# Router rows turned by DMA transposes, and sums of squares added on TensorE, in a fused attention and two-layer mixture kernel

## The chip, the cores and the metric

The kernel runs on one core of a Trainium2 chip. The metric is the device time of the whole program in microseconds (us), lower is better. TensorE multiplies matrices and transposes through PSUM; VectorE, ScalarE and GpSimd work on SBUF (GpSimd does not touch PSUM); SyncE (SP) issues most of the transfers. Each engine works through its own queue in order and waits on semaphores of the others.

## What is computed

```python
a = softmax(scale * x @ state.T);  xread = a @ state        # 8 batches, 8 heads, 512 tokens, 32 states, 64 wide
a2 = softmax(scale * state @ x.T); sread = a2 @ x
t = concat(xread, sread)            # -> 4352 tokens x 512
h = t @ w_in;  y = leaky_relu(h, 0.01) @ w_out               # 512 -> 2048 -> 512
logits = y @ w_gate; e = argmax(logits); p = softmax(logits)[e]
g = sigmoid(y @ w_output_gate)[e]
out = p * g * (relu(y @ w1[e]) @ w2[e])                      # 8 experts, 512 -> 1024 -> 512
```

Inputs and output are float32. The kernel splits values in two parts (fp32r pairs in the first layer, fp16 pairs in the router and the experts) and multiplies high by high, high by low and low by high.

## The kernel before

The first layer runs in nine chunks: eight x chunks (c = 0 to 7), one batch of 512 tokens each, and one chunk of the 256 state tokens (c = 8). Each has 16 steps (f = 0 to 15), one for each 128 hidden features, numbered n = 0 to 143 over all chunks. The order of the work is written out by hand in one loop over n. In a step come, in this order: `mm1(n)` (hidden features, with ScalarE's scaled copy, VectorE's max, and a split into `gh` and `gl`), in chunk 0 a piece of the conversion of the weights from 64-bit form (`convert`), a piece of the next batch's attention (`attend`), one advance of the expert weights' split (`advance(pre)`), `mm2(n - 2)` (three matmuls for each of four token tiles, accumulated over the chunk in PSUM), and `pump()`, one advance of the router of the chunk before.

The split of the expert weights (`presplit`) goes over 32 jobs of two tiles each and has four stages a job. The first squares tile 0 on ScalarE (`squares`, line 93, with a sum for each partition); the second squares tile 1, and GpSimd adds the two sums into a bf16 column (`suw`, line 643); the third sums over the partitions by a matmul with ones on TensorE (`over_partitions`, line 138), from which VectorE makes a power of two (`norm_scale`), and splits tile 0 (`halve`: VectorE lines 625 and 626, GpSimd line 627); the fourth stores tile 0 and splits tile 1, which the next job's first stage stores. It begins at n = 14 with one stage a step; in the last x chunk, from f = 2 on, two stages are advanced in one step, both ahead of `mm2`.

The gates' weights are loaded at n = 2; `gate_weights` squares, sums and splits them at n = 14 (lines 141 to 149).

The router of a chunk begins when `mm2` of f = 15 has been issued, in step f = 1 of the next chunk. Copies and squares of y (`evacuate`) come first. Then, at one `pump` each: `halves` of tile 0, of tile 1; then, for each of the four tiles, the logits of the tile before, `turn` of the tile (8 transposes on TensorE into PSUM, one copy on ScalarE into `yT`), and `halves` two tiles ahead; then softmax, choice and a scatter of the rows into the sorted table in DRAM. `pump` comes once a step, twice in the state chunk from f = 3 on, and twice in each expert slot (37 slots of 128 rows follow the first layer). The router of c = 7 runs in the state chunk; that of the state tokens (two tiles) runs in the first slots.

The pool of tag "y" (`r_p`, two buffers) holds y of two token tiles at a time, and early on the raw pieces of w_in.

Of the kernel before, what the change touches and what calls it, by code (L numbers as in the profile page):

```python
# [9 lines left out]
FP32 = mybir.dt.float32  # L10
FP32R = mybir.dt.float32r
FP16 = mybir.dt.float16
BF16 = mybir.dt.bfloat16
I32 = mybir.dt.int32
ACTF = mybir.ActivationFunctionType
ALU = mybir.AluOpType
# [7 lines left out]
def tile_attention_moe_moe2(ctx, tc, x, state, w_in, w_out, w_gate, w_ogate, w1, w2, out):  # L24
    nc = tc.nc
    B, H, S, D = x.shape
    NS = state.shape[2]
    DM, FF = w_in.shape
# [64 lines left out]
    def squares(o, t):  # L93

        k, n = t.shape[1:]
        nc.scalar.activation(out=junk[:, 0:k * n].rearrange("p (k n) -> p k n", n=n), in_=t, func=ACTF.Square,
                             scale=2.0 ** 0.5, accum_out=o)

    def norm_scale(pool, ss, s, inv):

# [21 lines left out]
    gwl = const.tile([128, KD, 2 * E], FP16, name="gwl")  # L122
    ginv = const.tile([128, 2], FP32, name="ginv")
    gsc = const.tile([128, 2], FP32, name="gsc")
    gss = const.tile([128, 2], FP32, name="gss")
    gsa = const.tile([128, 2], FP32, name="gsa")
    gsb = const.tile([128, 2], BF16, name="gsb")
    einv = const.tile([128, 2, 2, E], FP32, name="einv")
    esc = const.tile([128, 2, 2, E], FP32, name="esc")

# [1 line left out]
        for i, w in enumerate((w_gate, w_ogate)):  # L132
            nc.sync.dma_start(gw32[:, i], w.rearrange("(k p) e -> p k e", p=128))

    def over_partitions(t):

        ps = psa.tile([128, t.shape[1]], FP32, tag="a", name="tot")
        nc.tensor.matmul(ps, ones16.bitcast(BF16), t, start=True, stop=True)
        return ps

    def gate_weights():
        for i in range(2):
            squares(gss[:, i:i + 1], gw32[:, i])
        nc.vector.tensor_copy(gsb, gss)
        nc.vector.tensor_single_scalar(out=gsa, in_=over_partitions(gsb), scalar=128.0, op=ALU.mult)
        norm_scale(const, gsa, gsc, ginv)
        for i in range(2):
            sl = slice(i * E, (i + 1) * E)
            parts16(gwh[:, :, sl], gwl[:, :, sl], gw32[:, i], gsc[:, i:i + 1])
# [224 lines left out]
    def advance(g):  # L374
        try:
            next(g)
            return True
        except StopIteration:
            return False
# [115 lines left out]
    def router(ys2, ss, rows, tok_cols):  # L495
# [10 lines left out]
            nc.gpsimd.tensor_copy(row[:, 2 * DM + 2:2 * DM + 4].bitcast(I32), tok_cols[t])  # L506

        def turn(t):
            pt = psa.tile([128, 2 * KD, 128], FP16, tag="a", name="pt16")
            for k in range(2 * KD):  # L510
                nc.tensor.transpose(pt[:, k, :], rows[t][:, k * 128:(k + 1) * 128], id16)
            yTs[t] = r_p.tile([128, 2 * KD, 128], FP16, tag="yT", name="yT", bufs=1)
            nc.scalar.copy(out=yTs[t], in_=pt)

        def logits(t):
            yT = yTs.pop(t)
            pl = psa.tile([128, 2 * E], FP32, tag="a", name="pl")
            n = 0
            for a, w in ((0, gwh), (0, gwl), (KD, gwh)):
                for k in range(KD):  # L520
                    nc.tensor.matmul(pl, yT[:, a + k, :], w[:, k, :], start=(n == 0), stop=(n == 3 * KD - 1))
                    n += 1
            nc.vector.tensor_copy(lg[:, t], pl)
# [3 lines left out]
        halves(1)  # L527
        yield
        for t in range(nt):
            if t:  # L530
                logits(t - 1)
            turn(t)
            if t + 2 < nt:
                halves(t + 2)
            yield
        yield
        logits(nt - 1)
        ge = rt.tile([128, nt, E], FP32, tag="ge", name="ge")
# [51 lines left out]
    def presplit():  # L590
# [40 lines left out]
        for n, (e, half, m) in enumerate(jobs):  # L631
            wd = w1d if m == 0 else w2d
            if last is not None:
                nc.sync.dma_start(*last)
            t1 = load(n, 1)
            if n >= SPARE:
                ahead(n + 2)
            ss = sm.tile([128, 2], FP32, tag="ss2w", name="ss2w")
            squares(ss[:, 0:1], t0)
            yield  # L640
            squares(ss[:, 1:2], t1)
            su = sm.tile([128, 1], BF16, tag="suw", name="suw")
            nc.gpsimd.tensor_tensor(out=su, in0=ss[:, 0:1], in1=ss[:, 1:2], op=ALU.add)
            yield
            sa = sm.tile([128, 1], FP32, tag="saw", name="saw")
            s = esc[:, m, half, e:e + 1]
            nc.vector.tensor_scalar(out=sa, in0=over_partitions(su), scalar1=128.0, scalar2=2.0 ** -94,
                                    op0=ALU.mult, op1=ALU.max)
            norm_scale(sm, sa, s, einv[:, m, half, e:e + 1])
            pc = halve(t0, s)  # L650
            if n == SPARE - 1:
                ahead(n + 1)
                ahead(n + 2)
            yield
            nc.sync.dma_start(wd[e, :, 2 * half], pc)
            t0 = load(n + 1, 0)
            last = wd[e, :, 2 * half + 1], halve(t1, s)
            yield
# [18 lines left out]
    def pump():  # L677
        while active:
            if advance(active[0]):
                return  # L680
            active.popleft()
# [235 lines left out]
    for n in range(len(steps) + DEPTH):  # L917
# [30 lines left out]
            lo_part = None  # L948
        if n == 2:
            load_gates()  # L950
        if n == NF - 2:
            gate_weights()
        drain(conv)
        if n + 2 >= NF:
            for _ in range(2 if c == B - 1 and f >= 2 else 1):
                advance(pre)
        if n == NF * B:
            drain(pre)
            weight_scales()
# [23 lines left out]
        if n < 4:  # L983
            attend()
        pump()
    ab.close()


# [96 lines left out]
```

## Time and profile before

| | us |
|---|---|
| median of 3 runs | 1255.15 (1254.58 to 1257.69) |
| the profiled execution, its own time | 1256.79 |
| its span, first to last instruction | 1255.0 |
| TensorE busy | 1186.8 |
| VectorE busy | 790.1 |
| ScalarE busy | 517.7 |
| GpSimd busy | 391.2 |

The profile is of one execution; its time lies 1.64 us above the median of the runs, and 1.79 us of it lie outside the span. Busy times are sums over the whole span, in which stages with different limits follow each other. The mean granted clock of TensorE was 0.981 of full.

### The profile page before, as it was taken

Reading aid. Unit: us, or ns where it says so; the run is one execution under the profiler, and the core shown is the slowest. Engines: PE = TensorE matmul, PEld = TensorE weight load, DVE = VectorE, ACT = ScalarE, POOL = GpSimd, SP = SyncE. Lnnn points to the kernel's source line nnn. Section 1 sums busy time; section 2 is a strip of 40 time slices with the busy share of each in tenths; the row PEclk is TensorE's granted clock in tenths of the full one; section 3 lists DMA queues with packets and bytes.
Section 4 is the critical chain, followed back from the end, with each engine's and each line's share of the span. In section 5 each row is a group of like instructions: output and inputs, shape, how many; then the busy total and the mean of one; then the engine's idle time right before and its main releaser. Section 6 shows DMA issues by size and latency. Waiting matters only on the chain. (4 is left out here: it accounts for less than half of the span.)

```text
span 1255.0 us, 24909 instructions
## 1 busy us (share of the span) xinstructions
PE 1186.8 (95%) x9606; PEld 884.2 (70%) x9606; DVE 790.1 (63%) x1632; ACT 517.7 (41%) x984; POOL 391.2 (31%) x322
## 2 busy tenths in 40 slices
PE   6888999999999999999999888999999999999995
PEld 4655777777777777777776667877777777777773
DVE  6998577676776785776776897854543333333332
ACT  5775554544544644544645544431111111111111
POOL 3876224124233333224233354121211111111110
PEclk8898999999999999999999998999999999999998
DMA  6744226235226325425326352053315711133510
GB/s 176 222 155 121 84 68 190 83 102 168 81 93 168 106 96 143 128 85 158 101 85 215 137 186 84 26 189 127 116 52 196 294 48 44 52 110 127 175 52 24
DMA packets 97226, 152.76 MB, mean 122 GB/s; under 512 B 44111, under 2 KB 60495, under 8 KB 97104
## 3 DMA queue, kind: packets, MB, share of 16 engines
q1 hardware_dynamic: 88224, 122.73, 30.8%
q0 software_dynamic: 8880, 28.40, 6.6%
q8 instruction: 77, 1.26, 0.4%
q14 instruction: 45, 0.37, 0.1%
HBM read 229.71 MB, written 52.20 MB: 225 GB/s over the span
## 5 line engine op out<-in xcount | busy, mean ns | idle before, releaser
L739 PE MATMUL y<-woh,gh 128*128 128x512 f32 x544 | 226.9, 417 | 0.0
L740 PE MATMUL y<-wol,gh 128*128 128x512 f32 x544 | 216.5, 398 | 0.0
L741 PE MATMUL y<-woh,gl 128*128 128x512 f32 x544 | 215.9, 397 | 0.0
L1009 PE MATMUL h<-xt,w1t 128*128 128x128 f16 x1184 | 200.4, 219 | 0.0
L1010 PE MATMUL h<-xt,w1t 128*128 128x128 f16 x1184 | 200.4, 219 | 0.0
L1011 PE MATMUL h<-xt,w1t 128*128 128x128 f16 x1184 | 200.4, 219 | 0.0
L627 POOL TENSOR_TENSOR pc<-raw,pc 128x1024 f16<-128x1024 f32 x54 | 129.1, 2391 | 168.9 <-issue 114.5
L722 DVE TENSOR_TENSOR u<-h,u 128x512 f32<-128x512 f32 (+1 forms) x144 | 94.7, 657 | 132.1 <-ACT u L721 132.0
L1015 ACT ACTIVATE r<-h,room 128x512 f32<-128x512 f32 x74 | 50.9, 687 | 253.5 <-PE h L1011 253.5
L1017 DVE TENSOR_SCALAR rh<-h,room 128x512 f16<-128x512 f32 x74 | 55.5, 750 | 125.5 <-ACT r L1015 125.5
L1044 POOL DMA_INDIRECT out_dram<-osb,ti x37 | 37.5, 1014 | 309.8 <-DVE ti L1042 309.2
L739 PEld LDWEIGHTS y<-woh,gh 128*128 128x128 f32 x544 | 104.9, 193 | 41.2 <-issue 12.3
L195 ACT CAST gh<-u 128x512 fp32r<-128x512 f32 (+1 forms) x144 | 85.6, 594 | 106.0 <-DVE u L722 105.8
L741 PEld LDWEIGHTS y<-woh,gl 128*128 128x128 f32 x544 | 104.4, 192 | 24.1
L1009 PEld LDWEIGHTS <-w1t 128*128 128x128 f16 x1184 | 115.8, 98 | 4.4 <-issue 0.3
L1010 PEld LDWEIGHTS <-w1t 128*128 128x128 f16 x1184 | 115.8, 98 | 4.1
L740 PEld LDWEIGHTS y<-wol,gh 128*128 128x128 f32 x544 | 104.9, 193 | 18.5
L196 DVE TENSOR_TENSOR gl<-u,gh 128x512 fp32r<-128x512 f32 (+1 forms) x144 | 108.2, 752 | 12.2 <-ACT gh L195 9.5
L1011 PEld LDWEIGHTS <-w1t 128*128 128x128 f16 x1184 | 115.8, 98 | 0.0
L721 ACT ACTIVATE u<-h 128x512 f32<-128x512 f32 (+1 forms) x144 | 82.4, 572 | 79.9 <-PE h L717 78.3
L1032 PE MATMUL o<-w2t,rh 128*128 128x512 f16 x296 | 112.2, 379 | 0.6 <-DMA w2t<-w2s 0.5
L1034 PE MATMUL o<-w2t,rl 128*128 128x512 f16 x296 | 112.2, 379 | 0.1
(226 smaller groups left out, 2297.7 us busy)
## 6 DMA issues: line engine op xcount, KB each, us to landing
w1t<-w1s SPq DMA_DIRECT2D x152, 512.0 KB
w2t<-w2s SPq DMA_DIRECT2D x152, 512.0 KB
raw<-in_moe_w_dram SPq DMA_DIRECT2D x54, 512.0 KB
w1s<-pc SPq DMA_DIRECT2D x32, 512.0 KB
w2s<-pc SPq DMA_DIRECT2D x32, 512.0 KB
x<-in_x_dram SPq DMA_DIRECT2D x32, 256.0 KB
wir<-in_moe_w_in_dram SPq DMA_DIRECT2D x16, 512.0 KB
wor<-in_moe_w_out_dram SPq DMA_DIRECT2D x16, 512.0 KB
```

What stands on the lines that cost most here:

```text
L195: nc.scalar.copy(out=h, in_=t)
L196: return lambda: nc.vector.tensor_tensor(out=l, in0=t, in1=h.bitcast(FP32), op=ALU.subtract)
L627: nc.gpsimd.tensor_tensor(out=pc[:, 1], in0=t, in1=pc[:, 0], op=ALU.subtract)
L722: nc.vector.tensor_tensor(out=u, in0=ps, in1=u, op=ALU.max)
L739: nc.tensor.matmul(ys[c][t], gh[:, sl], woh[f], start=(f == 0), stop=False)
L740: nc.tensor.matmul(ys[c][t], gh[:, sl], wol[f], start=False, stop=False)
L741: nc.tensor.matmul(ys[c][t], gl[:, sl], woh[f], start=False, stop=(f == NF - 1))
L1009: nc.tensor.matmul(ps[:, i, :], wh, xt[:, k, :], start=(k == 0), stop=False)
L1010: nc.tensor.matmul(ps[:, i, :], wh, xt[:, KD + k, :], start=False, stop=False)
L1011: nc.tensor.matmul(ps[:, i, :], wl, xt[:, k, :], start=False, stop=(k == KD - 1))
L1032: nc.tensor.matmul(ps, h, w2t[q][:, 0, fi, :], start=(f == 0), stop=False)
L1034: nc.tensor.matmul(ps, l, w2t[q][:, 0, fi, :], start=False, stop=(f == KF - 1))
```

## The change

`turn` no longer uses TensorE and ScalarE: a transposing DMA on SP's queue reads the halves of a tile from SBUF and writes `yT` into a buffer of the space of y, two tiles to a buffer. The logits of a tile come two advances of the router behind its turn, where they came one behind; the number of advances is the same. The squares' sums are written as bf16 columns; GpSimd's addition is gone, and the ones-matmul takes the two columns one after the other into the same PSUM column. The squares of the gates move to n = 12 and the rest of the gates' work to n = 13. In the last x chunk the second advance of the weights' split in a step moves behind `mm2` and `pump`.

```diff
     def squares(o, t):
...
-        nc.scalar.activation(out=junk[:, 0:k * n].rearrange("p (k n) -> p k n", n=n), in_=t, func=ACTF.Square,
-                             scale=2.0 ** 0.5, accum_out=o)
+        with nc.allow_low_precision(reason="of the sum only the exponent is used"):
+            nc.scalar.activation(out=junk[:, 0:k * n].rearrange("p (k n) -> p k n", n=n), in_=t, func=ACTF.Square,
+                                 scale=2.0 ** 0.5, accum_out=o)
...
-    gss = const.tile([128, 2], FP32, name="gss")
+    gss = const.tile([128, 2], BF16, name="gss")
...
-    def over_partitions(t):
-
-        ps = psa.tile([128, t.shape[1]], FP32, tag="a", name="tot")
-        nc.tensor.matmul(ps, ones16.bitcast(BF16), t, start=True, stop=True)
+    def over_partitions(*cols):
+
+        ps = psa.tile([128, cols[0].shape[1]], FP32, tag="a", name="tot")
+        for i, t in enumerate(cols):
+            nc.tensor.matmul(ps, ones16.bitcast(BF16), t, start=(i == 0), stop=(i == len(cols) - 1))
         return ps
 
-    def gate_weights():
+    def gate_squares():
         for i in range(2):
             squares(gss[:, i:i + 1], gw32[:, i])
-        nc.vector.tensor_copy(gsb, gss)
-        nc.vector.tensor_single_scalar(out=gsa, in_=over_partitions(gsb), scalar=128.0, op=ALU.mult)
+
+    def gate_weights():
+        nc.vector.tensor_single_scalar(out=gsa, in_=over_partitions(gss), scalar=128.0, op=ALU.mult)
...
         def turn(t):
-            pt = psa.tile([128, 2 * KD, 128], FP16, tag="a", name="pt16")
-            for k in range(2 * KD):
-                nc.tensor.transpose(pt[:, k, :], rows[t][:, k * 128:(k + 1) * 128], id16)
-            yTs[t] = r_p.tile([128, 2 * KD, 128], FP16, tag="yT", name="yT", bufs=1)
-            nc.scalar.copy(out=yTs[t], in_=pt)
+            if t % 2 == 0:
+                yTs["both"] = r_p.tile([128, 2, 2 * KD, 128], FP16, tag="y", name="yT")
+            yTs[t] = yTs["both"][:, t % 2]
+            nc.sync.dma_start_transpose(out=yTs[t], in_=rows[t][:, 0:2 * DM])
...
         for t in range(nt):
-            if t:
-                logits(t - 1)
+            if t > 1:
+                logits(t - 2)
             turn(t)
             if t + 2 < nt:
                 halves(t + 2)
             yield
+        logits(nt - 2)
         yield
         logits(nt - 1)
...
-            ss = sm.tile([128, 2], FP32, tag="ss2w", name="ss2w")
+            ss = sm.tile([128, 2], BF16, tag="ss2w", name="ss2w")
             squares(ss[:, 0:1], t0)
             yield
             squares(ss[:, 1:2], t1)
-            su = sm.tile([128, 1], BF16, tag="suw", name="suw")
-            nc.gpsimd.tensor_tensor(out=su, in0=ss[:, 0:1], in1=ss[:, 1:2], op=ALU.add)
             yield
...
-            nc.vector.tensor_scalar(out=sa, in0=over_partitions(su), scalar1=128.0, scalar2=2.0 ** -94,
+            nc.vector.tensor_scalar(out=sa, in0=over_partitions(ss[:, 0:1], ss[:, 1:2]), scalar1=128.0, scalar2=2.0 ** -94,
...
-        if n == NF - 2:
+        if n == NF - 4:
+            gate_squares()
+        if n == NF - 3:
             gate_weights()
         drain(conv)
         if n + 2 >= NF:
-            for _ in range(2 if c == B - 1 and f >= 2 else 1):
-                advance(pre)
+            advance(pre)
...
         pump()
+        if c == B - 1 and f >= 2:
+            advance(pre)
```

## Rows read from the trace of the kernel before

**Rows 1.** Windows: length, busy us of PE, PEld, DVE, ACT, POOL, clock, DMA.
```profile
145.00:669.00 524.00, 518.64 (x3320) 384.12 (x3319) 380.14 (x827) 271.17 (x530) 168.36 (x129) 1.00 0.39 118
687.00:769.00 82.00, 69.06 (x374) 51.76 (x373) 70.28 (x127) 40.93 (x72) 38.29 (x27) 0.94 0.44 155
829.00:1240.00 411.00, 410.06 (x4793) 304.45 (x4794) 167.70 (x326) 77.38 (x121) 76.19 (x74) 1.00 0.33 117
```
**Rows 2.** Waits of PE, whole span: us in total, times, longest.
```profile
PE tot L138 <- POOL suw L643: 14.5, 9, 4.1
PE tot L138 <- DVE gsb L144: 5.3, 1, 5.3
```
**Rows 3.** Timeline of PE, chunk 1: start, us, engine, line, operation, count.
```profile
160.91 0.61 PE L511 MATMUL pt<-id,row 128*128 128x128 f16 x8
161.33 0.48 PE L715 MATMUL h<-a1h,kh 128*128 128x512 f32 x1
```
**Rows 4.** Timeline of SP and PE at the start; DMA queues of the page.
```profile
1.84 2.93 SPq L209 DMA_DIRECT2D x<-in_x_dram  x4
5.18 0.90 PE L238 MATMUL bank<-id,x 128*128 128x128 f32 x3 [0.80 <-DMA x<-in_x_dram]
...
q1 hardware_dynamic: 88224, 122.73, 30.8%
```
**Rows 5.** Timelines of DVE, SP and PE, chunk 2, its router.
```profile
237.99 0.75 DVE L111 SCALAR_TENSOR_TENSOR row<-y,s,row 128x512 f16<-128x512 f32 x1
...
261.05 0.39 SPq L613 DMA_DIRECT2D raw<-in_moe_w_dram  x1
...
274.90 0.26 PE L521 MATMUL pl<-gwh,yT 128*128 128x16 f16 x4
```
**Rows 6.** Timeline of the state chunk, router of the last x chunk.
```profile
784.43 0.75 DVE L111 SCALAR_TENSOR_TENSOR row<-y,s,row 128x512 f16<-128x512 f32 x1
...
790.60 0.75 DVE L111 SCALAR_TENSOR_TENSOR row<-y,s,row 128x512 f16<-128x512 f32 x1
...
796.74 0.26 PE L521 MATMUL pl<-gwh,yT 128*128 128x16 f16 x4
```
**Rows 7.** Timeline of PE, chunk 1, around a ones-matmul.
```profile
157.72 0.18 PE L138 MATMUL tot<-suw,ones 128*128 128x1 bf16 x1
157.76 0.47 PE L739 MATMUL y<-woh,gh 128*128 128x512 f32 x1
...
160.60 0.26 PE L521 MATMUL pl<-gwh,yT 128*128 128x16 f16 x4
```
**Rows 8.** Timeline of the last x chunk; in brackets idle time and its releaser.
```profile
691.84 0.19 ACT L96 ACTIVATION_READ_ACCUMULATOR junk<-x 128x1 f32 x1
...
692.36 0.16 PE L138 MATMUL tot<-suw,ones 128*128 128x1 bf16 x1 [4.10 <-POOL suw L643]
...
717.35 0.99 ACT L513 COPY yT<-pt 128x1024 f16<-128x1024 f16 x1
...
718.87 0.69 DVE L722 TENSOR_TENSOR u<-h,u 128x512 f32<-128x512 f32 x1 [2.36 <-ACT u L721]
...
728.76 0.18 ACT L96 ACTIVATION_READ_ACCUMULATOR junk<-x 128x1 f32 x1
...
729.63 0.20 ACT L560 ACTIVATE z<-z 128x4 f32<-128x4 f32 x1 [0.56 <-DVE z L559]
```
**Rows 9.** Timelines of PE and ACT in chunk 0, n = 12 to 15.
```profile
109.86 0.50 PE L739 MATMUL y<-woh,gh 128*128 128x512 f32 x1
...
110.08 0.62 ACT L195 CAST gh<-u 128x512 fp32r<-128x512 f32 x1
...
119.88 0.23 ACT L96 ACTIVATE junk<-junk 128x32 bf16<-128x32 f32 x1
...
120.82 0.18 PE L138 MATMUL tot<-gsb,ones 128*128 128x2 bf16 x1 [5.25 <-DVE gsb L144]
...
125.98 0.40 PE L715 MATMUL h<-a1h,kh 128*128 128x512 f32 x1
```

More of the change, by code (lines that the diff above doesn't have):

```diff
@@ L124, in tile_attention_moe_moe2 @@
     gsc = const.tile([128, 2], FP32, name="gsc")
-    gss = const.tile([128, 2], FP32, name="gss")
+    gss = const.tile([128, 2], BF16, name="gss")
     gsa = const.tile([128, 2], FP32, name="gsa")
-    gsb = const.tile([128, 2], BF16, name="gsb")
     einv = const.tile([128, 2, 2, E], FP32, name="einv")
```

## The prediction

> **What bounds the kernel now.** I read the windows first, stage by stage, because the busy share of the whole span mixes stages with different limits. From 145 to 669 us TensorE is busy for 518.64 of 524 us at full clock: that stretch, in which the second to seventh chunks run, is bound by TensorE, and time taken off its queue there comes off the end. From 829 us to the end (the expert slots) it is busy for 410.06 of 411. Between 687 and 769 us, the last x chunk, it is busy for only 69.06 of 82 us, while VectorE is busy for 70.28: something else sets the pace there [rows 1]. The chain of work that ended last is no help: it holds two steps. So I went to TensorE's waits. The list is short: the ones-matmul of the weight splits waits 14.5 us for GpSimd's sum, in nine places, and that of the gates waits 5.3 us for a VectorE cast, in one [rows 2]. Asked by stretch, nearly all of the 14.5 us lies in the last x chunk. Then I read the timelines around each wait and around one router tile.
>
> **Router tiles on TensorE.** A tile is 8 transposes. They start at 160.91, and the next matmul starts at 161.33: 0.42 us [rows 3], far below 8 times the 219 ns of one, since they are pipelined. Of the 34 tiles, 24 are turned in the stretch that TensorE bounds (chunks 1 to 6, four each): 24 x 0.42 = 10.1 us come off. The other end is the length of the eight in the same row, 0.61 us: 14.6 us. The two tiles of state tokens, turned in the slots, give 2 x 0.42 = 0.8 us more, for the slots are bound by TensorE as well [rows 1].
>
> A rule speaks against the move. The row shows TensorE turning a 128x128 block each 0.05 us when eight stand in a stream [rows 3]. The Trainium skill ("VectorE: DVE Perf Modes", section "The three transpose paths") puts one such block at 390 ns on TensorE and 1309 ns by the DMA crossbar, and advises TensorE where the result may go to PSUM. The row decides for the TensorE side. An estimate by that page alone, eight blocks in series, is 10.5 us a tile on the DMA; what that would do is a rival below.
>
> **Are the turned rows there in time?** No row shows a transposing DMA. The nearest is a plain one of the same 256 KB: SP begins to issue it at 1.84 us and its first reader starts at 5.18, so 3.3 us with the issue [rows 4]. That is my value and the lower bound. For the upper one: the hardware queue's 88,224 packets took 30.8% of 16 engines' span, 70 ns each [rows 4]; if a tile went as 1,024 pieces of 256 B, 64 an engine, that is 4.5 us on top, 7.8 us in all (an estimate from that row). SP takes its work in order, so each issue also stands behind the stores and loads ahead of it. In the chunk from 233 us rows 0 are ready at 238.74. The latest is the fourth tile: SP reaches it behind the store and the load at 261.05, so at 261.4, and its logits start at 274.90 now, some 1.7 us sooner without the four turns [rows 5]. About 11.8 us of slack against 3.3 to 7.8: hidden, cost nothing, in chunks 1 to 7. If the cover were gone, each us of lateness would be one of TensorE's, per chunk. SP has idle time for 34 more issues: it waits for GpSimd's halves in that chunk and nothing on the path waits for it. What stands behind a turn on SP is the next step's store, which waits for GpSimd longer anyway.
>
> In the chunk of state tokens the router of the last x chunk advances twice a step, so two steps ahead is about one of its short steps. There TensorE waits now for VectorE's rows and for ScalarE's copy. Rows 0 are complete at 785.18 and rows 3 at 791.35; the last logits start at 796.74 [rows 6]. With 3.3 us a tile the fourth lands at 794.7 and TensorE, behind its step's matmuls, gets to it at about 795.2: 1.5 us sooner. I take 1.0, with -2.3 and +3.5 (at 7.8 us a tile the fourth lands at 799.2) as ends.
>
> **The ones-matmul with two columns.** Each of 32 now is two. One with a single column starts at 157.72 and the next matmul at 157.76, 0.04 us [rows 7]; its weight load is not hidden each time, so I take 0.055 for the extra one: 24 in the stretch bound by TensorE, +1.3 us (0.04 to 0.10: 1.0 to 2.4).
>
> **GpSimd's sum.** What goes is the hop, not the wait. At 691.84 ScalarE begins to read out the second sum, done at 692.03; the matmul starts at 692.36 after 4.10 us of idle time [rows 8]. Without the hop it can start at about 692.1: 0.3 of 4.1 us. The rest is ScalarE's own lateness: its squares stand behind a cast that waits for VectorE's max. The two such waits before 675 us (1.5 us in all) lose the same hop: 0.5 us.
>
> **The last x chunk.** The second advance moves behind the matmuls of y, but a step's work on each engine keeps its order: the squares still stand before the next step's copy on ScalarE. The cycle of two steps runs from VectorE's max, through both halves (one slowed to 2.5 us beside GpSimd), the next max, a cast, two squares, ScalarE's copy and again the max; TensorE's sum is not on it. Two edits touch it. In two cycles the copy of a turned tile stands in the chain, 0.99 us each, and VectorE idles 2.36 us for what follows: -2.0. In the step of the router's exponentials the second squares now stand behind them. They ended at 728.94, the exponential that is last ended at 729.83 [rows 8], and squares with read-out take 1.2 us: the chain ends some 1.4 us later than it did. Sum -0.6; as ends I take -4 (the shorter hop in seven cycles, and order gained) and +4 (the later halves of the second tile delay the next step).
>
> **The gates.** TensorE reaches this point at n = 14 and stands still for 5.25 us, since ScalarE's two squares are behind casts of the conversion, and VectorE's cast behind those. Then the granted clock is at the 1.2 GHz level: the ones-matmul and twelve others from 120.82 to 125.98 take 5.16 us, where at the 2.4 GHz level they took 2.88 (157.72 to 160.60) [rows 7, 9]. After: the squares follow the cast of n = 12, which ends at 110.70. From the first square to the matmul it is 0.94 us (119.88 to 120.82) with VectorE's cast, so 0.7 without, and TensorE reaches the place of n = 13 at 109.86 [rows 9]. So a wait of some 1.6 us stays. Whether the clock stays up behind so short a one none of these rows shows; I take it that it does. Gain 5.25 - 1.6 + 2.3 = 6.0 us; 3.6 if the clock falls anyway, 7.6 if no wait stays.
>
> **Sum**, against the profiled execution (span 1255.0, own time 1256.79): -10.1 (turns) + 1.3 (second columns) - 0.5 (hop) - 6.0 (gates) - 0.6 (last x chunk) - 1.0 (state chunk) - 0.8 (slots) = -17.7 us, so 1239.1. The median, 1255.15, lies 1.6 us lower: 1237.5, and I say 1238. With all good ends -30, with all bad ones -5.
>
> **Rivals.** (a) The forecast, 0.62. (b) The waits for GpSimd in the last x chunk go whole, with the drop of the clock behind the 4.1 us one. For: the wait list names GpSimd. Against: ScalarE ends just before it each time. That is 14.5 less the 0.5 counted, most of it: 1225; 0.13. (c) The gates' wait stays nearly whole, one step earlier, and the last chunk gets longer: 1246 to 1250; 0.14. (d) The stretch from 145 us has a second engine just behind TensorE, so only the gates are won: 1250 to 1254, no change or little; 0.05. Against it: VectorE is busy for 380 of 524 us there [rows 1]. (e) Slower: a turned tile occupies the DMA queue for a time T, one after the other. From rows 0 ready (238.74) to the last logits (273) four fit if T is below 8.6 us; in the state chunk four would end at 785.2 + 4T, against 796.7 now. At T = 7.3 that costs 17.7 us, all that was won, and that is the point from which it decides; at T = 10, seven chunks lose 5.7 us each and the state chunk 30: 1238 + 70 = 1308. For it: no row shows such a transfer. Against: the plain one takes 3.3 us [rows 4]; 0.06. The Trainium skill's rule ("VectorE: DVE Perf Modes", section "The three transpose paths") is this rival's: its estimate of 10.5 us a tile would give about 1320.
>
> **Numbers.** Likeliest 1238. The range 1228 to 1250 takes in (a), most of (c) and a part of (b); outside lie the rest of (b), (d) and (e), about 0.2. A measurement of this kernel tells about 0.3% (3.8 us) from no change: faster 0.89, same 0.05, slower 0.06.
>
> **What would show it.** Right: no transposes of the router on TensorE; the logits hardly wait for a DMA before 675 us; chunks 1 to 6 each some 1.7 us shorter; the wait of the gates' matmul under 2 us with the clock up; waits of the ones-matmul in the last x chunk nearly as long as before, now ended by ScalarE; one of them longer, in the step after the exponentials. Wrong: logits that wait for the turned tiles in every chunk; SP's stores and raw loads landing late, with ScalarE's squares waiting for them; the last x chunk shorter by ten us.

## The result, and the profile after

The changed kernel takes 1241.08 us, the median of 4 runs (1239.17 to 1242.77), the kernel before beside it 1256.32 (4 runs): ratio 0.9881, 95% interval 0.9863 to 0.9899. The profiled execution took 1242.63 us, with a span of 1240.9.

To see where the 14.1 us of span went I cut both profiles at the same marks: ScalarE's first copy of y of chunk 0, of chunk 6 and of chunk 7, TensorE's first matmul of the slots, GpSimd's last scatter. "Last x chunk" is the piece between the second and the third mark, "state chunk" the one from there to the slots. Where ScalarE waits for the buffer of a copy, the mark is the copy itself and not the wait.

| | start to first mark | chunks 1 to 6 | last x chunk | state chunk | slots |
|---|---|---|---|---|---|
| before | 142.09 | 538.70 | 98.72 | 51.57 | 410.82 |
| after | 137.25 | 525.92 | 98.90 | 55.59 | 410.16 |
| difference | -4.84 | -12.78 | +0.18 | +4.02 | -0.66 |

Windows of before, cut at these marks (columns as in [rows 1]):

```profile
680.79:779.51 98.72, 84.02 (x452) 63.80 (x451) 84.03 (x151) 47.68 (x90) 47.42 (x38) 0.95 0.42 150
779.51:831.08 51.57, 47.47 (x369) 41.46 (x368) 35.61 (x120) 24.96 (x58) 8.74 (x10) 1.00 0.22 80
```

Windows of after:

```profile
137.25:663.17 525.92, 522.10 (x3222) 386.42 (x3221) 388.94 (x845) 256.49 (x520) 165.17 (x108) 1.00 0.48 136
663.17:762.07 98.90, 84.28 (x423) 63.84 (x422) 83.00 (x151) 44.20 (x86) 44.92 (x31) 0.90 0.49 160
762.07:817.66 55.59, 48.61 (x340) 41.79 (x338) 35.69 (x119) 21.26 (x53) 8.80 (x10) 0.96 0.34 102
817.66:1227.82 410.16, 408.77 (x4766) 302.95 (x4765) 167.46 (x326) 74.72 (x118) 75.98 (x74) 1.00 0.32 115
```

In the third row, the state chunk, TensorE has lost its four turns and is busy for longer all the same, 48.61 against 47.47 us, at a mean granted clock of 0.96 against 1.00; and it idles for 6.98 us against 4.10. The last x chunk is as long as before, at 0.90 against 0.95. In the state chunk the clock is at its lower level, 1.2 GHz (0.50), in a stretch behind a wait that ends at 774.86 us (the wait for a turned tile, below):

```profile
776.00:778.00 2.00, 2.00 (x14) 1.28 (x13) 0.09 (x2) 0.92 (x2) 0.00 (x0) 0.50 0.97 188
```

TensorE's waits of after, whole span, beside [rows 2]:

```profile
PE tot L139 <- ACT junk L97: 12.3, 8, 4.1
PE tot L139 <- DVE u L722: 5.6, 6, 1.8
...
PE pl L522 <- DMA yT<-row: 3.2, 1, 3.2
PE t L890 <- DMA row<-srt,room: 2.9, 1, 2.9
...
PE h L717 <- DVE kl L194: 2.3, 1, 2.3
```

The sum's waits are nearly all still there (12.3 against 14.5 us) and now named ScalarE's, as predicted. The logits wait for a turned tile once in 34, in the state chunk. In the x chunks the tiles are early by a wide margin. VectorE, SP and TensorE in the chunk of [rows 5], which begins 6.7 us earlier now: rows 0 and rows 1, the first and the last of the four turns, and the logits of the first and the last tile:

```profile
231.31 0.75 DVE L112 SCALAR_TENSOR_TENSOR row<-y,s,row 128x512 f16<-128x512 f32 x1
...
234.29 0.75 DVE L112 SCALAR_TENSOR_TENSOR row<-y,s,row 128x512 f16<-128x512 f32 x1
...
235.11 1.73 SPq L514 DMA_TRANSPOSE yT<-row  x1
...
248.55 0.26 PE L522 MATMUL pl<-gwh,yT 128*128 128x16 f16 x4
...
254.25 1.90 SPq L514 DMA_TRANSPOSE yT<-row  x1
...
266.31 0.26 PE L522 MATMUL pl<-gwh,yT 128*128 128x16 f16 x4
```

The last turn is issued about when I had reckoned. The first goes out not behind rows 0 (complete at 232.06) but behind rows 1 (235.04), 3 us later than reckoned. Even so 12 to 13 us lie between an issue and its reader, and nothing waits. The gates, beside [rows 9]:

```profile
112.55 0.16 PE L139 MATMUL tot<-gss,ones 128*128 128x2 bf16 x1 [1.38 <-DVE cv L183]
112.57 0.48 PE L739 MATMUL y<-woh,gh 128*128 128x512 f32 x1
...
115.40 0.39 PE L715 MATMUL h<-a1h,kh 128*128 128x512 f32 x1
```

The wait is 1.38 us where 1.6 was predicted, and the ones-matmul and its twelve followers take 2.85 us (112.55 to 115.40), at the 2.4 GHz level (the granted clock is 1.00 from 112 to 116 us), where they took 5.16.

### The profile page after: what moved, and what is told of

It reads as the page before. It is cut to its first block, busy times and chain, and to the rows that moved or that the text cites. A ratio compares the mean times of both kernels' runs of the same rounds, so it can differ in the third digit from the quotient of the medians.

```text
span 1240.9 us, 24399 instructions
## 1 busy us (share of the span) xinstructions
PE 1173.9 (95%) x9366; PEld 874.0 (70%) x9366; DVE 788.4 (64%) x1631; ACT 486.6 (39%) x950; POOL 380.4 (31%) x290
## 3 DMA queue, kind: packets, MB, share of 16 engines
q1 hardware_dynamic: 124128, 131.65, 35.5%
## 5 line engine op out<-in xcount | busy, mean ns | idle before, releaser
L1018 ACT ACTIVATE r<-h,room 128x512 f32<-128x512 f32 x74 | 50.8, 687 | 258.0 <-PE h L1014 258.0
L198 DVE TENSOR_TENSOR gl<-u,gh 128x512 fp32r<-128x512 f32 (+1 forms) x144 | 108.6, 754 | 12.1 <-ACT gh L197 10.3
```

What stands on the lines that cost most here:

```text
L198: return lambda: nc.vector.tensor_tensor(out=l, in0=t, in1=h.bitcast(FP32), op=ALU.subtract)
```

## The experiments

They ran on three other chips, on which the kernel before takes 1264 to 1266 us; b2 below shows where. Times are therefore compared as ratios to the kernel before on the same chip, and profiles by the pieces ahead of the slots. The pieces are those of one execution; the six executions of the changed kernel in a2 lie 11 us apart (1246.29 to 1257.53 us), the 17 of the kernel before beside e1 5 us. This table has them all (first mark, pieces as above, ratio with interval):

| run | first mark | chunks 1-6 | last x | state | ratio |
|---|---|---|---|---|---|
| after | 137.3 | 525.9 | 98.9 | 55.6 | 0.9881 (0.9863-0.9899) |
| a2: after, again | 139.7 | 526.6 | 94.4 | 56.0 | 0.9894 (0.9870-0.9918) |
| b2: before, again | 141.6 | 537.9 | 98.7 | 50.9 | |
| e1: turns only | 142.1 | 528.4 | 95.9 | 51.9 | 0.9908 (0.9893-0.9922) |
| e2: all but turns | 136.8 | 537.7 | 100.6 | 54.8 | 1.0007 (0.9996-1.0018) |
| e3: advance as before | 136.6 | 527.2 | 97.7 | 54.4 | 0.9888 (0.9867-0.9909) |
| e7: advance ahead of router | 138.2 | 527.0 | 97.7 | 53.0 | 0.9892 (0.9874-0.9909) |
| e9: e3 with GpSimd's sum | 138.6 | 525.9 | 97.3 | 50.8 | 0.9857 (0.9842-0.9872) |
| e4: after, own buffer | 136.2 | 526.4 | 98.9 | 53.7 | 0.9864 (0.9847-0.9881) |
| e8: e3, own buffer | 138.8 | 526.5 | 95.3 | 50.7 | 0.9870 (0.9855-0.9884) |
| e10: e9, own buffer | 136.8 | 527.4 | 97.4 | 50.3 | 0.9853 (0.9836-0.9871) |
| e5: TensorE turns in state chunk | 136.7 | 525.7 | 98.1 | 52.7 | 0.9895 (0.9877-0.9912) |
| e11: waits filled | 138.0 | 525.8 | 96.7 | 53.2 | 0.9871 (0.9857-0.9885) |

The expectations of e3 and e10 give the stretch from the copy of chunk 6 to the first slot matmul as 155.0 us in the changed kernel, 148.4 in e1 and 148.6 in e9; they count from where ScalarE begins to wait for that copy's buffer. From the copy it is 154.5, 147.9 and 148.1.

**The turns alone, and all the rest alone.** My first theory (T) was that the turns bring the gain and also the growth of the state chunk. e1 puts into the kernel before only this:

```diff
         def turn(t):
-            pt = psa.tile([128, 2 * KD, 128], FP16, tag="a", name="pt16")
-            for k in range(2 * KD):
-                nc.tensor.transpose(pt[:, k, :], rows[t][:, k * 128:(k + 1) * 128], id16)
-            yTs[t] = r_p.tile([128, 2 * KD, 128], FP16, tag="yT", name="yT", bufs=1)
-            nc.scalar.copy(out=yTs[t], in_=pt)
+            if t % 2 == 0:
+                yTs["both"] = r_p.tile([128, 2, 2 * KD, 128], FP16, tag="y", name="yT")
+            yTs[t] = yTs["both"][:, t % 2]
+            nc.sync.dma_start_transpose(out=yTs[t], in_=rows[t][:, 0:2 * DM])
...
-            if t:
-                logits(t - 1)
+            if t > 1:
+                logits(t - 2)
```

> The kernel before with the router's rows turned by DMA, two steps ahead of their use, and nothing else of the change: the squares, GpSimd's sum, the gates and the second advance stand as before. Measured so far: before 1256.3, after 1241.1 us; between the two profiles the stretch of chunks 1 to 6 lost 12.8 us, the stretch from the last ones-matmul of the splits to the first slot matmul grew by 5.2 us. Theory T (the turns give the gain and the growth): chunks 1 to 6 shorter by 12 to 15 us (a little more than in the changed kernel, which pays for second ones-matmul columns), state chunk longer by some 5, slots shorter by 0.8, the gates' wait still 5.3: 1246 to 1249. Rival H (the growth comes from the second advance that was moved, and a part of the gain from GpSimd's hop): chunks 1 to 6 shorter by about 10, state chunk no longer than before: 1244 to 1246. The stretches tell them apart better than the time.

e2 is the changed kernel with this diff taken back.

> The changed kernel with the router's rows turned on TensorE one step ahead of their use, as before; all else changed. Theory T: the gates give 4.8, the last x chunk about 1, the second columns cost about 1 in chunks 1 to 6, the state chunk keeps its old length of 64.6 us between its two landmarks: 1250 to 1253. Rival H (the moved second advance lengthens the state chunk): that stretch is near 70 us and the time 1255 to 1257.

Both fell on the rival's side. e1: ratio 0.9908, which is 1244.7 of the first 1256.3 us; chunks 1 to 6 are 9.5 to 10.3 us shorter (against b2 and before) and the state chunk only 0.4 to 1.1 us longer, though the logits wait 2.9 us there. e2: ratio 1.0007. The gates' gain is there (first mark at 136.8), the state chunk has grown by 3.3 to 4.0 us, the last x chunk by 1.9, and nothing is left. So the turns are worth 11.6 us net (0.0092 of 1256.3), and all the rest together, put into the kernel before, nothing. Windows of the last x chunk and the state chunk, e1:

```profile
670.51:766.45 95.94, 81.56 (x419) 61.63 (x418) 81.59 (x151) 43.99 (x85) 47.46 (x38) 0.95 0.52 165
766.45:818.39 51.94, 47.38 (x338) 41.41 (x337) 35.76 (x120) 21.27 (x54) 9.10 (x10) 0.97 0.31 93
```

and e2:

```profile
674.47:775.08 100.61, 85.53 (x455) 65.00 (x454) 82.24 (x151) 47.99 (x89) 45.48 (x31) 0.92 0.41 147
775.08:829.91 54.83, 49.90 (x372) 43.42 (x371) 35.86 (x119) 25.02 (x57) 8.84 (x10) 0.97 0.25 89
```

What a turn costs TensorE can be read from the chunks: an undisturbed one of e1 takes 87.84 us from mark to mark where before's takes 89.77, 1.93 us for four turns, so 0.48 each. [rows 3] shows 0.42 for the second tile of its chunk. The first tile stands ahead of another matmul, which starts 0.56 us behind the first transpose (before):

```profile
153.56 0.62 PE L511 MATMUL pt<-id,row 128*128 128x128 f16 x8
154.12 1.08 PE L474 MATMUL kps<-w,stf 128*64 128x256 f32 x8
```

Two tiles of each of the six chunks are of this kind and two of the other. 24 turns at 0.48 are 11.6 us; e1 wins 9.5 to 10.3, since its ones-matmuls wait for GpSimd's sum for 2.7 us in two of the six chunks (1.13 and 1.57), where in before they wait for 1.55 (1.12 and 0.43).

**The place of the second advance.** With theory T gone I blamed the advance that was moved (M). e3 puts it back, e7 moves it only ahead of the router's step:

```diff
# e3
-            advance(pre)
+            for _ in range(2 if c == B - 1 and f >= 2 else 1):
+                advance(pre)
...
-        if c == B - 1 and f >= 2:
-            advance(pre)
# e7
+        if c == B - 1 and f >= 2:
+            advance(pre)
         pump()
-        if c == B - 1 and f >= 2:
-            advance(pre)
```

> The changed kernel with the second advance of the weight splits in the last x chunk back in its old place, ahead of the matmuls of y. The four runs so far have turned theory T around: with the turns alone the stretch from the last chunk-6 copy landmark (first ScalarE copy of y of chunk 6) to the first slot matmul is 148.4 us, with all but the turns 155.4, in the changed kernel 155.0, before 150.3; TensorE's clock is at its lower level for 27 us of it in the changed kernel and 10 before. Theory M (the moved second advance makes new waits of 2 to 3 us, with the clock at its lower level behind them): that stretch falls to 148 to 150 us, the time by 5 to 6 us, to 1235 to 1236 (ratio to before near 0.984). Rival C (the ones-matmul with two columns in place of GpSimd's sum does it): the stretch stays at 154 to 155 and the time at 1241.

> The changed kernel with the second advance behind the matmuls of y, but ahead of the router's step, so that the second squares stand ahead of the router's exponentials as before the change. Theory M2 (what costs is only the order against the router's exponentials): the wait of 2.5 us in the step behind the exponentials goes to about 1.3, with no drop of the clock behind it: 2 to 3 us less, 1238 to 1239. Theory M (the place behind the matmuls of y costs as such): the other waits stay, so that no more than those 2 to 3 us come back. Rival C: no change, 1241.

Neither moved the time: 0.9888 and 0.9892, beside 0.9881 and 0.9894 for the changed kernel. In the step behind the exponentials the wait did fall, from 2.45 to about 0.6 us, as M2 and the prediction have it. But waits of 1.0 us in pairs, one for each of the two columns, stand in other steps instead: ScalarE's waits sum to 11.9 and 11.8 us in that chunk (nine each). The gains that M (a ratio near 0.984) and M2 expected lie outside both intervals, so M and M2 are refuted.

**GpSimd's sum.** e9 is e3 with the sum on GpSimd and the single ones-matmul back, so that of the whole change only the turns and the gates are left:

```diff
-            ss = sm.tile([128, 2], BF16, tag="ss2w", name="ss2w")
+            ss = sm.tile([128, 2], FP32, tag="ss2w", name="ss2w")
...
             squares(ss[:, 1:2], t1)
+            su = sm.tile([128, 1], BF16, tag="suw", name="suw")
+            nc.gpsimd.tensor_tensor(out=su, in0=ss[:, 0:1], in1=ss[:, 1:2], op=ALU.add)
...
-            nc.vector.tensor_scalar(out=sa, in0=over_partitions(ss[:, 0:1], ss[:, 1:2]), scalar1=128.0, scalar2=2.0 ** -94,
+            nc.vector.tensor_scalar(out=sa, in0=over_partitions(su), scalar1=128.0, scalar2=2.0 ** -94,
```

> The changed kernel with GpSimd's sum of the two squares and the single ones-matmul kept, and the second advance in its old place: only the turns and the gates are changed. Theory M: the stretch from the chunk-6 copy to the first slot matmul is 148 to 149 us as with the turns alone, chunks 1 to 6 are 0.5 to 1.5 us shorter than in the changed kernel, for want of the second columns, the gates' gain of 5 stays: 1235 to 1237. Rival C (the two-column matmul is what lengthens the last stretches): 5 us less than the kernel with only the advance put back. If both are equal, the removed hop was worth nothing.

Rival C has it: 1248.55 against 1252.48 us on the same chip, ratios 0.9857 and 0.9888 (their intervals just overlap). Chunks 1 to 6 are 1.3 us shorter than in e3 and the state chunk 3.7 us. In the second to fourth of the six chunks, where the two kernels wait alike, e9 is shorter by 0.15 to 0.18 us each: that is the price of four second columns. The rest of the 1.3 us is waits of other ones-matmuls, which come and go from one execution to the next. Windows of e9's last x chunk and state chunk:

```profile
664.47:761.73 97.26, 81.89 (x419) 61.66 (x418) 81.69 (x151) 43.98 (x85) 47.44 (x38) 0.95 0.51 162
761.73:812.52 50.79, 46.07 (x339) 40.16 (x337) 35.76 (x120) 21.25 (x54) 9.31 (x10) 1.00 0.31 93
```

and e3's:

```profile
663.76:761.46 97.70, 83.48 (x423) 63.44 (x422) 82.34 (x151) 44.21 (x85) 46.68 (x31) 0.93 0.50 162
761.46:815.90 54.44, 48.22 (x341) 41.48 (x339) 35.82 (x120) 21.26 (x53) 9.53 (x10) 0.96 0.32 100
```

The waits of TensorE in the state chunk, e9:

```profile
PE pl L522 <- DMA yT<-row: 2.8, 1, 2.8
PE t L892 <- DMA row<-srt,room: 1.0, 1, 1.0
PE y L743 <- DVE gl L198: 0.9, 1, 0.9
```

and e3:

```profile
PE pl L522 <- DMA yT<-row: 3.2, 1, 3.2
PE t L890 <- DMA row<-srt,room: 2.1, 1, 2.1
PE y L741 <- DVE gl L198: 0.9, 1, 0.9
```

The waits are 1.5 us longer in e3, and TensorE is busy for 2.15 us longer, at 0.96 against 1.00. In the last x chunk the sum's waits are 14.0 us in e9 and 11.9 in e3, and the chunk is no shorter. At the first step of the state tokens' matmuls, where TensorE waits for VectorE's split of the weights, it waits 1.3 us in e9 and 2.2 in e3, and it is busy for 1.6 us longer in e3, at 0.93 against 0.95.

**The buffer of the turned tile.** In the state chunk the first turn is late. After, VectorE and SP:

```profile
767.89 0.75 DVE L112 SCALAR_TENSOR_TENSOR row<-y,s,row 128x512 f16<-128x512 f32 x1
...
770.35 0.75 DVE L112 SCALAR_TENSOR_TENSOR row<-y,s,row 128x512 f16<-128x512 f32 x1
...
771.25 4.86 SPq L514 DMA_TRANSPOSE yT<-row  x3
...
774.86 0.26 PE L522 MATMUL pl<-gwh,yT 128*128 128x16 f16 x4 [3.19 <-DMA yT<-row]
```

Rows 0 are complete at 768.64, but the turn goes out at 771.25, when rows 1 are (771.10): the "space of y" that it writes is the buffer from which rows 1 are still being made. e4 gives the first and third tile 2 KB of their own:

```diff
         def turn(t):
             if t % 2 == 0:
-                yTs["both"] = r_p.tile([128, 2, 2 * KD, 128], FP16, tag="y", name="yT")
-            yTs[t] = yTs["both"][:, t % 2]
+                yTs[t] = r_p.tile([128, 2 * KD, 128], FP16, tag="yT", name="yT", bufs=1)
+            else:
+                if t == 1:
+                    yTs["odd"] = r_p.tile([128, 2 * KD, 128], FP16, tag="y", name="yT")
+                yTs[t] = yTs["odd"]
```

> The changed kernel, but the first and third turned tile of a router go to a buffer of their own of 2 KB, and the second and fourth share one in the space of y, so that the first turn need not wait until rows 1 have been halved, nor the third until rows 3 have. Theory B (the state chunk lost its 5.2 us because the first turn was held by the buffer): the first turn is issued some 2.6 us sooner, the logits' wait of 3.2 us goes to under 1 us, the time falls by 2.5 to 4 us to 1237 to 1238.5. Rival D (it is the transfer itself, 3.6 us in short steps, wherever it begins): the logits wait elsewhere for as long and the time stays within 1 us of 1241. In chunks 1 to 6 neither expects a difference.

The mechanism holds. VectorE and SP in e4:

```profile
767.35 0.75 DVE L112 SCALAR_TENSOR_TENSOR row<-y,s,row 128x512 f16<-128x512 f32 x1
...
768.17 6.16 SPq L517 DMA_TRANSPOSE yT<-row  x3
```

and TensorE's waits there:

```profile
PE t L893 <- DMA row<-srt,room: 3.3, 1, 3.3
PE y L744 <- DVE gl L198: 0.9, 1, 0.9
PE pl L525 <- DMA yT<-row: 0.7, 2, 0.5
```

The turn goes out 0.07 us behind rows 0, the logits wait 0.7 us instead of 3.2, the state chunk is 1.9 us shorter than in after and 2.3 than in a2; a part is waited for again at the first slot (3.3 against 2.9 us). The ratio, 0.9864, is below both of the changed kernel's, but not clear of either interval. The same buffer in e3 (e8) and in e9 (e10):

> The old place of the second advance together with the buffer of its own for the first and third turned tile. Theory M with theory B: the stretch from the chunk-6 copy to the first slot matmul is 146 to 148 us and the time 1233 to 1234 (ratio near 0.982), since the wait for the turned tile (2.9 us with the turns alone) goes to under 1 us. Rival D (the transfer itself holds the logits wherever the turn is issued): as with the old place alone.

> Turns by DMA with the first and third tile in a buffer of their own, the early gates, GpSimd's sum and the single ones-matmul kept, the second advance in its old place. With the sum kept and the turned tiles in the space of y the stretch from the chunk-6 copy to the first slot matmul was 148.6 us and the ratio to before 0.9857. Theory B (the buffer holds the first turn back): 2 to 3 us less in that stretch, 145.5 to 146.5, ratio 0.983 to 0.985. Rival L (the last stretch is set by the chain behind the router, rows to the scratch store and back, and what is won ahead of it is waited for at the first slot): stretch 148 and ratio 0.9855.

e8 wins 3.8 us of the state chunk but 0.0018 of the ratio, inside the intervals, where a ratio near 0.982 was expected; e10 wins 0.5 us and 0.0004, nothing: rival L's case. e8 and e10 differ by GpSimd's sum alone, and their state chunks by 0.4 us: with the buffer of its own, taking the sum out lengthens that stretch hardly at all. Turning the four tiles of the last x chunk's router on TensorE again (e5; `done` counts the routers begun), with the other 30 on the DMA, is no way out:

```diff
+        pe = len(rows) == 4 and len(done) == B
...
+            if pe:
+                pt = psa.tile([128, 2 * KD, 128], FP16, tag="a", name="pt16")
+                for k in range(2 * KD):
+                    nc.tensor.transpose(pt[:, k, :], rows[t][:, k * 128:(k + 1) * 128], id16)
+                yTs[t] = r_p.tile([128, 2 * KD, 128], FP16, tag="yT", name="yT", bufs=1)
+                nc.scalar.copy(out=yTs[t], in_=pt)
+                return
...
-            if t > 1:
+            if pe:
+                if t:
+                    logits(t - 1)
+            elif t > 1:
                 logits(t - 2)
```

> The changed kernel, but the router of the last x chunk, which runs in the short steps of the chunk of state tokens, turns its four tiles on TensorE one step ahead as before; the other routers keep the DMA. Theory T (the growth of that stretch is due to the turned tiles' lateness): the stretch returns to about 64.6 us, the wait for the turned tile is gone, the time is 1236 to 1238. Rival H (the moved second advance or the later clock drop has made that stretch longer): it stays near 70 us and the time at 1241 to 1243, since four turns more stand on TensorE.

The ratio is 0.9895: nothing is won, as rival H has it. In the profile the wait for the DMA is gone, a wait for ScalarE's copy (1.6 us) and the turns themselves take its place, and the state chunk is 2.9 us shorter than in after, at a clock of 1.00; but the profiled execution is one of three near 1247 us, and the other three took 1252.

**The clock.** e11 fills five of TensorE's long waits with matmuls that are used by nothing: ahead of the first or second column of three splits, of the first logits of the last x chunk's router, and of the first transposes of the slots:

```diff
+    def fill(room, n):
+        for j in range(n):
+            k = 128 * (j % 3)
+            nc.tensor.matmul(room[:, k:k + 128], ones16, id16, start=True, stop=True)
...
+                ss[:, 0:1], ss[:, 1:2], fills={25: (40, 0), 28: (0, 40), 30: (60, 0)}.get(n, (0, 0))), scalar1=128.0, scalar2=2.0 ** -94,
...
+            if t == 0 and len(done) == B:
+                fill(room, 50)
...
+        for k in range(0 if b else 50):
+            nc.tensor.transpose(pt[:, k % 8, :], id16, id16)
```

> The changed kernel with matmuls of the identity put into TensorE's five longest waits of the last two stretches: 40 ahead of the first column of split 25, 40 between the two columns of split 28, 60 ahead of split 30, 50 ahead of the first logits of the last x chunk's router, 50 ahead of the first transposes of the slots; at some 0.055 us each they take 2 to 3.3 us at full clock. They compute nothing that is used. Theory K (the changed kernel pays for the lower clock behind its waits, 27 us of it in that stretch of 155): the mean granted clock there rises from 0.90 and 0.95 to 0.95 or more, and the stretch loses 3 to 7 us. Rival W (the waits themselves are the price, the clock's drops fall into time that is waited for anyway): the clock rises, the stretch stays within 1 us or grows by the 1 to 3 us by which fillers outlast the waits.

The control on the same chip:

> The changed kernel, unaltered, on the chip of these runs, since chips differ in the slots: 410 us of them on the chip of the first comparison, 419 to 423 in the experiments. Theory M (the second advance behind the matmuls of y costs 2 to 3 us against its old place): ratio to before 0.990 to 0.992 here, above the 0.989 of the kernel with the advance put back. If the place makes no difference: 0.988 to 0.989.

a2's ratio, 0.9894, lies between the two values expected, and its interval holds both, so it does not settle what the advance's place costs. The state chunk's window in a2:

```profile
760.73:816.71 55.98, 48.85 (x341) 42.00 (x339) 35.93 (x119) 21.24 (x53) 8.90 (x10) 0.95 0.34 104
```

and in e11:

```profile
760.49:813.68 53.19, 51.63 (x439) 45.75 (x437) 35.76 (x120) 21.25 (x54) 8.77 (x10) 1.00 0.36 104
```

With the clock at 1.00 the state chunk is 2.8 us shorter than in a2 (53.2 against 56.0), although TensorE is given more to do. The medians point the same way, 1250.42 against 1254.11 us, with intervals that overlap a little (0.9857 to 0.9885, 0.9870 to 0.9918). So theory K holds for the state chunk, as far as one profile of each can show it. For the whole stretch that the expectation names it is not settled: from the copy of chunk 6 to the first slot matmul e11 takes 149.9 us, after 154.5 and a2 150.4, so that against a2 rival W's number came true. The last x chunk differs between two executions of the same kernel: 98.9 in after, 94.4 in a2. Most of that is one thing. VectorE and GpSimd in after:

```profile
729.43 3.68 DVE L933 TENSOR_TENSOR srl<-srT,srh 128x512 fp32r<-128x512 f32 x2
...
730.39 2.17 POOL L629 TENSOR_TENSOR pc<-xT,pc 128x1024 f16<-128x1024 f32 x1
...
736.08 0.16 PE L139 MATMUL tot<-ss2w,ones 128*128 128x1 bf16 x1 [4.06 <-ACT junk L97]
```

and in a2:

```profile
730.49 1.28 DVE L933 TENSOR_TENSOR srl<-srT,srh 128x512 fp32r<-128x512 f32 x2
...
734.73 0.16 PE L139 MATMUL tot<-ss2w,ones 128*128 128x1 bf16 x1 [1.15 <-ACT junk L97]
```

Two subtractions on VectorE take 3.68 us when GpSimd's subtraction runs beside the second, 1.28 when it doesn't, and the ones-matmul behind them waits 4.06 or 1.15 us. Of the 14 profiles only those of a2 and e11 escape this meeting. The Trainium skill ("GPSIMD Engine Reference", section "1. Specifications") says that GpSimd shares its interfaces to SBUF with VectorE and contends with VectorE's instructions with two SBUF inputs; these rows agree.

**The kernel before, for the chips.** b2 is unaltered.

> The kernel before, unaltered, for its profile on the chip of these runs. If the slots differ by chip and not by kernel: 419 to 423 us from the first slot matmul to the last scatter, the chunks as on the first chip (89.8 us each). If the slots of the experiments were longer because of their edits: 411 us.

Its slots:

```profile
830.00:1252.00 422.00, 415.72 (x4768) 299.38 (x4765) 165.26 (x326) 76.00 (x119) 76.20 (x74) 1.00 0.31 111
```

They take 423.1 us there and 410.8 on the first chip, for the same instructions at the same clock, with 6 us of TensorE's idle time where [rows 1] has 1 and 5.7 us more of its busy time; the other pieces agree within 0.8 us. So it goes with the chip and not with the edits; why is open. a2's slots (422.4) gain the same 0.7 us as after's.

## Why the prediction was right, and where it was not

The time, 1241.08, lies 3 us above the 1238 predicted and inside its range. That it came so near is in part luck, for errors of opposite sign cancel: chunks 1 to 6 gave 3.5 us more than the terms laid there (-12.8 against -10.1 + 1.3 - 0.5), the state chunk 5.0 us less, the gates 1.2 and the last x chunk 0.8 less. By its terms:

- **The turns in chunks 1 to 6** (-10.1). Right in the mechanism, too small in size: 0.48 us a turn where [rows 3] gave 0.42, for the prediction took one kind of tile for both, so 11.6 us in all. The changed kernel wins 12.8 us in this stretch (11.4 from b2 to a2): after has none of the waits for GpSimd's sum there, and its last chunk takes 86.30 us, as in all eight profiles with turns by DMA and without that sum, where e1's takes 88.04.
- **The second columns** (+1.3). Too much: 0.15 to 0.18 us for four of them (e3 against e9), so 0.04 each and some 1.0 us for 24. The 0.055 us, for a weight load that is not hidden each time, no run shows: in before each of the 32 ones-matmuls is followed by the next matmul within 0.04 us.
- **The hop** (-0.5). The two waits for GpSimd's sum ahead of 675 us, 1.12 and 0.43 us in before, are gone in after: -1.5. In b2 there is one, of 0.87, so a part of that is chance.
- **Hidden transfers** (0). Right: no logits wait before the state chunk. From the issue at 771.25 to the reader at 774.86 a tile takes 3.6 us, in e4 3.1 (768.17 to 771.27), where 3.3 was assumed. It went as 1,056 packets, near the 1,024 of the upper bound, but without the 4.5 us on top. So rival (e) and the Trainium skill's 1309 ns a block ("VectorE: DVE Perf Modes", section "The three transpose paths"; 10.5 us a tile as an estimate) do not describe these tiles of eight blocks; another page of it does ("Advanced Engine Details and Errata", section "X-Bar Transpose (TRN2)": transposing DMAs are as fast as regular ones), against the 3.3 us of the plain transfer [rows 4].
- **The gates** (-6.0): -4.8 in the profile, the wait and the clock as predicted. At the place itself 6.2 us are won (the wait 3.9, the clock 2.3); behind it the first ones-matmul of the weight splits waits longer, 1.79 us where it waited 0.76. The first mark scatters (136.2 to 139.7 in eleven profiles with early gates, 141.6 to 142.1 in three without); e9 against e1, whose only difference they are, gives 0.0051, 6.4 us, with intervals that lie apart. Rival (c) is out.
- **The last x chunk** (-0.6): +0.2 in the profile, -4.3 from b2 to a2, of which a2 alone escapes the meeting of the subtractions, so no gain or loss that can be put down to the change. The step behind the exponentials waits longer, as foreseen (1.33 before, 2.45 after), and e7 shows no gain from undoing it. That the waits for GpSimd's sum are ScalarE's lateness, so that rival (b) fails, the changed kernel shows itself: without the sum 12.3 of the 14.5 us are still waited for.
- **The state chunk** (-1.0, ends -2.3 and +3.5). This is the step that failed: +4.0 (+5.1 from b2 to a2), beyond its worse end. I took rows 0 as the only condition of the first turn and did not ask whose buffer it writes, so I put the tile too early; and I gave the other edits no part in this stretch. The runs put the buffer at 1.9 to 2.3 us in the changed kernel (e4) and at 3.8 beside the old advance (e3 against e8). They put the hop's removal, which I had priced as a small gain, at 3.7 (e3 against e9; with the moved advance 3.3 to 4.0, e2 against before and b2), but at 0.4 where the tile has its own buffer (e8 against e10). The two do not add up, for what costs is largely common to both: TensorE waits two or three times for 2 to 3 us, and works at the lower clock level for a time afterwards (0.50 from 776 to 778 us in after). At 0.96 over 55.6 us some 2.2 us are lost (55.6 x 0.04), near the 2.5 by which TensorE is busy longer than in e9 with the same matmuls at 1.00; the idle time grew by 2.9 over before, and e11 gets 2.8 back by filling the waits. These prices are differences of single profiles; in the ratios only e3 against e9 is told from nothing, and barely.
- **The slots** (-0.8): -0.7.

Step by step from before to a2, in ratios times 1256.3 us: turns -11.6 (e1), gates -6.4 (e1 to e9), the ones-matmul in place of GpSimd's sum +3.9 (e9 to e3), the advance's new place +0.8, which the intervals do not tell from nothing (e3 to a2): -13.3. The steps were taken on three chips, and each is known to some 2 us; in another order they are worth something else, for all but the turns is +0.9 alone (e2) and -1.7 on top of the turns. The best kernels are e9 and e10, some 18 us below before: the change without its ones-matmul edit, with the second advance in its old place. On one chip e10 took 1247.72 us and the changed kernel 1254.11.

What stays open: why TensorE's wait for the first slot's rows is 0.8 to 1.0 us in e1, e7 and e9 and 2 to 3.3 in e2, e3, e4 and the changed kernel, and how much of the hop's price is the clock's chance. e8, without GpSimd's sum, waits 2.2 us for the split of the weights and 2.0 for the first slot's rows, keeps the clock at 1.00, and has a state chunk of 50.7 us.

## What to carry to other kernels

Where TensorE bounds a stage, as in chunks 1 to 6 here, a stream of transposes that a DMA does well ahead of its reader (12 us ahead, for a transfer of 3.1 to 3.6) comes off the time. Where TensorE waits for other engines it need not, and there ask whose buffer the moved transfer writes: a borrowed one brings its last reader along as a new wait. Price a stream by each of its neighbours, not by one. A hop that is taken out ahead of a waiting engine is worth only what the chain behind it lets through: follow the wait to the next place before booking a gain. Near the end of such a chain price a wait of 2 to 3 us with what the clock does behind it, cut all profiles at the same event, and look at a second execution before reading a difference of a few microseconds as an effect.

## What the runs showed of the hardware

- A transposing DMA of 128 x 1024 fp16 from SBUF to SBUF holds SP's queue for 1.2 to 2.8 us (median 1.5 of 34, in after), makes 1,056 packets ((124,128 - 88,224) / 34) and is read 3.6 us after its issue begins (after) or 3.1 (e4), where the logits wait for it; a turn of the same tile costs TensorE 0.48 us on the mean (e1 against before).
- The length of a wait alone does not tell whether the clock falls behind it. The state chunk kept 1.00 with a wait of 2.83 us in e9 and had 0.97 with one of 2.85 in e1; the gates' 1.38 us in after left it up.
- Chips differ: the slots of the kernel before took 410.8 us on one chip and 423.1 on another (b2), at the same granted clock.
